# Chunk attention and a token-mixing MLP on one core: q and k loaded unit by unit with four rows in a partition, and one projection transposed in pairs of chunks

## The chip, the cores and the metric

The kernel runs on one core of one Trainium2 chip. The metric is the device time of one execution in microseconds (us). Before the change the median of three runs is 151.93 us (151.79 to 152.24). A further execution, the one whose profile is shown, took 152.53 us.

## What is computed

The inputs are q, k and v, each of 8 batches x 8 heads x 576 tokens x 64 columns in float32, and three weights: w_q and w_k (512 x 64) and w_out (512 x 512). The result is 8 x 576 x 512 in float32.

```python
# attention inside chunks of 64 tokens
scores = scale * np.matmul(q_c, k_c.transpose(0, 1, 2, 4, 3))
attn = softmax(scores)                 # with 1e-09 added to the sum
out = np.matmul(attn, v_c)
# then, with x = the heads side by side: batch x token x 512
wq, wk = x @ w_q, x @ w_k
W_tok = (1 / 8) * wq @ wk.T            # 576 x 576 per batch
result = np.maximum(W_tok @ x, 0.0) @ w_out
```

A head has nine chunks, a batch 72, and no chunk sees another. The MLP mixes all tokens of a batch; the kernel computes it as wq (wk^T x), so that the 576 x 576 matrix is never formed.

## The kernel before, in words

**Tiling.** The heads of a batch are split into two slabs of four heads. A slab fills 64 of the 128 partitions or 64 columns, so that two chunks, one of each slab, are worked on side by side. There are 36 such pairs of chunks in a batch (`NI`), and a *unit* is eight of them: 36 units (`NU`) in all, four and a half to a batch.

**Stages of a unit.** `stage_a1` transposes q and k on TensorE (PE) by 16 matmuls with an identity (line 375), so that the head's 64 columns come to lie on partitions; `stage_a2` copies the result from PSUM to SBUF on VectorE (DVE, line 385). `stage_b1` multiplies q by k (PE, line 400) and takes the maximum of each row (DVE, line 408); `stage_b2` subtracts it (DVE, line 414) and takes the exponential on ScalarE (ACT, line 422). `stage_c` transposes the result (PE, line 429; ACT copy, line 431). `stage_d1` multiplies by v, which has a column of ones for the sum (PE, line 445); `stage_d2` divides by the sum (DVE, lines 457, 459 and 460) and leaves a slice of x in SBUF.

**Rows in a partition.** q and k come with `R` = 2 neighbouring tokens in one partition (line 89): one contiguous piece of 128 float32 numbers in HBM becomes 128 float16 numbers in SBUF. The tokens of a chunk are thus held in the order (r g), r of 2 and g of 32, and not in their own order. That is undone for the keys where line 414 writes its result (`sh`, float32, as (g r)), and for the queries where the MLP's relu reads PSUM as (g r) (lines 267 and 287).

**Loads.** All loads are DMAs that GpSimd's queue (POOL) issues, because they cast from float32 to float16. `load_qk(b, part)` loads four or five of the nine half-units of a batch, with a DMA for each slab and each of q and k, so four DMAs. `load_v(b, part)` loads 8 or 10 of 18 chunk pairs with three DMAs (line 101) after a memset of the ones (line 98). Lines 119 to 125 issue two batches of q and k ahead of the first unit, with three parts of v among them. After that `reload` (line 506) issues the load of batch b + 2 when the same part of batch b has been used up; each part has two buffers. The weights come in behind the first reloads (`also`, line 501).

**Order.** The order on every engine is the order of the program. Lines 524 to 543 are the loop over units: in step kk, `stage_b1` of unit kk, `stage_d1` of unit kk - 2, `stage_a1` of unit kk + 2, `stage_c` of unit kk - 1, `stage_b2` of kk, `stage_d2` of kk - 2, `stage_a2` of kk + 2. The steps of a batch's MLP (`make_moe`) are put between them by a plan with places and costs (lines 472 to 498). One of them is `p_wkn` (line 204): it turns the projection wk, which lies as 64 rows x 576 tokens, by transposes of 64 x 64 (line 215), two for each of nine pairs of chunks, 18 in a batch. Slot n holds chunk 2n in partitions 0 to 63 and chunk 2n + 1, modulo nine, in partitions 64 to 127. After the last unit, lines 561 to 594 run what is left of batches 5, 6 and 7.

Of the kernel before, what the change touches and what calls it, by code (L numbers as in the profile page):

```python
# [9 lines left out]
F16 = mybir.dt.float16  # L10
# [7 lines left out]
def kernel(  # L18
# [12 lines left out]

    nc = tc.nc
    B, H, S, D = q.shape
    DM = moe_w_out.shape[0]
    DH = moe_w_q.shape[1]
    CH = 64
    P = 128
    HQ = H // 2  # L40
    NC_ = S // CH
    NI = HQ * NC_
    NT = NI // 4
    NS = NI // 2
    NU = B * NI // 8
    W0 = 5 * CH
    R, G = 2, 32
    scale_attn = 1.0 / math.sqrt(D)
    scale_moe = 1.0 / math.sqrt(DH)
    ds = bass.ds  # L50

    const = ctx.enter_context(tc.tile_pool(name="const", bufs=1))
    qn_pool = ctx.enter_context(tc.tile_pool(name="qn", bufs=2))
    v_pool = ctx.enter_context(tc.tile_pool(name="vpool", bufs=2))
    qkt_pool = ctx.enter_context(tc.tile_pool(name="qkt", bufs=3))
    sm_pool = ctx.enter_context(tc.tile_pool(name="smp", bufs=3))
# [14 lines left out]
    ident = const.tile([P, P], F16, name="ident")  # L71
# [5 lines left out]
    wqk16 = const.tile([P, HQ, 2 * DH], F16, name="wqk16")  # L77
    wout16 = const.tile([P, HQ, DM], F16, name="wout16")


    cuts = ((0, 4), (4, NT))
    v_cuts = ((0, 8), (8, NS))
    data = {}

    def load_qk(b, part):
        t0, t1 = cuts[part]
        for ti, x in enumerate((q, k)):
            tl = qn_pool.tile([P, 2, t1 - t0, R * D], F16, name=f"qn{ti}{part}", tag=f"qn{ti}{part}")
            of = x[b].rearrange("h s d -> (h s) d").rearrange("(l t p r) d -> l p t (r d)", l=2, p=P, r=R)
            for sl in range(2):  # L90
                nc.gpsimd.dma_start(tl[:, sl], of[sl, :, t0:t1, :])  # L91
            data[b, part, ti] = tl

    def load_v(b, part):
        n0, n1 = v_cuts[part]
        vt = v_pool.tile([P, 2, n1 - n0, D + 2], F16, name=f"vt{part}", tag=f"vt{part}")
        of = v[b].rearrange("h s d -> (h s) d").rearrange("(l n p) d -> l p n d", l=2, p=P)
        nc.gpsimd.memset(vt[:, :, :, D : D + 1], 1.0)

        for sl, to, at, rows in ((0, 0, 0, P), (1, 0, CH, CH), (1, CH, 0, CH)):  # L100
            nc.gpsimd.dma_start(vt[to : to + rows, sl, :, 0:D], of[sl, at : at + rows, n0:n1, :])  # L101
        data[b, part, 2] = vt
# [13 lines left out]

    load_qk(0, 0)
    load_qk(0, 1)  # L120
    load_v(0, 0)
    load_qk(1, 0)
    load_v(0, 1)
    load_qk(1, 1)
    load_v(1, 0)

    drain = [False]
    taken = [0]
# [1 line left out]
    def bank(shape, dtype, name):  # L130

        taken[0] += 1
        if drained() and taken[0] % 6 == 0:
            return s_psum.tile(shape, dtype, name=name, tag="sp")
        return m_psum.tile(shape, dtype, name=name, tag="m")

    def drained():
        return drain[0]

    def copy(on_vector, to, of):  # L140
        (nc.vector.tensor_copy if on_vector else nc.scalar.copy)(to, of)  # L141
# [9 lines left out]
    def make_moe(b):  # L151
# [52 lines left out]
        def p_wkn():  # L204


            wk = st["wqkT"][CH:P]
            wkn = moe_pool.tile([P, NC_, DH], F16, name="wkn", tag="wkn")

            cuts_ = (0, 5, NC_) if b == B - 1 else (0, NC_)  # L210
            for n0, n1 in zip(cuts_, cuts_[1:]):
                wp = bank([P, n1 - n0, DH], F16, name="wknp")
                for n in range(n0, n1):
                    for o in range(2):
                        nc.tensor.transpose(
                            wp[CH * o : CH * o + CH, n - n0, :],
                            wk[:, ds((2 * n + o) % NC_ * CH, CH)],
                            ident[CH:P, CH:P],
                        )
                copy(n0 > 0, wkn[:, n0:n1], wp[:])  # L220
            st["wkn"] = wkn
# [135 lines left out]
            outs.insert(0 if b == B - 1 else 4, (2, 0.9, p_out_tail))  # L357
        return xts[:2], chain, outs

    def batch_of(gj):  # L360
        return divmod(gj, NT)

    state = {}

    def stage_a1(u):

        tp = bank([P, 2, 2, 4, R, G], F16, name="tp")
        for j in range(2):
            b, t = batch_of(2 * u + j)
            for ti in range(2):  # L370
                part = t >= cuts[1][0]
                src = data[b, part, ti][:, :, t - cuts[part][0]]
                for r in range(R):
                    for sl in range(2):
                        nc.tensor.transpose(  # L375
                            tp[CH * sl : CH * sl + CH, j, ti, :, r, :],
                            src[:, sl, r * D : r * D + D],
                            ident[:],
                        )
        state[u] = {"tp": tp}  # L380

    def stage_a2(u):
        tp = state[u]["tp"]
        qkt = qkt_pool.tile([P, 2, 2, 4, R * G], F16, name="qkt", tag="qkt")
        nc.vector.tensor_copy(  # L385
            qkt[:].rearrange("p j t c k -> p (j t c k)"),
            tp[:].rearrange("p j t c r g -> p (j t c r g)"),
        )
        state[u]["qkt"] = qkt

    def stage_b1(u):


        qkt = state[u]["qkt"]
        sp = s_psum.tile([P, 8, CH], F32, name="sp", tag="sp")
        for i in range(8):
            j, c = divmod(i, 4)
            for sl in range(2):
                rows = slice(CH * sl, CH * sl + CH)
                nc.tensor.matmul(  # L400
                    sp[rows, i ^ sl, :],
                    lhsT=qkt[rows, j, 0, c, :],
                    rhs=qkt[rows, j, 1, c, :],
                    start=True,
                    stop=True,
                )
        mx = sm_pool.tile([P, 8], F32, name="mx", tag="mx")
        nc.vector.tensor_reduce(mx[:], sp[:], axis=AX.X, op=ALU.max)  # L408
        state[u]["sp"], state[u]["mx"] = sp, mx
# [24 lines left out]
    def stage_d1(u):  # L434
        et = state[u]["et"]
        xp = x_psum.tile([P, 2, 512], F32, name="xp", tag="xp")
        xv = xp[:, :, 0 : 4 * 65].rearrange("p l (m e) -> p l m e", e=65)
        for m in range(4):
            b, s = divmod(4 * u + m, NS)
            part = s >= v_cuts[1][0]  # L440
            vt = data[b, part, 2][:, :, s - v_cuts[part][0]]
            for sl in range(2):
                for par in range(2):
                    at = CH * (par ^ sl)
                    nc.tensor.matmul(  # L445
                        xv[CH * par : CH * par + CH, sl, m, :],
                        lhsT=et[at : at + CH, m, CH * sl : CH * sl + CH],
                        rhs=vt[at : at + CH, sl, 0 : D + 1],
                        start=True,
                        stop=True,  # L450
                    )
        state[u]["xv"] = xv
# [40 lines left out]
    def fill(kk, place, budget):  # L493
        spent = sum(run(x) for x in plan.pop((kk, place), []))
        while outs and outs[0][0] == place and spent + outs[0][1] <= budget:
            _, cost, step = outs.pop(0)
            step()
            spent += cost


    also = {
        (load_qk, 2, 0): [load_wqk, lambda: load_v(1, 1)],
        (load_qk, 2, 1): [load_wout],
    }

    def reload(load, unit, per_unit, per_batch, ends):

        for x in range(per_unit * unit + 1, per_unit * unit + per_unit + 1):
            b, end = divmod(x, per_batch)
            b, end = (b, end) if end else (b - 1, per_batch)  # L510
            for part in range(2):
                if end == ends[part][1] and b + 2 < B:
                    load(b + 2, part)
                    for more in also.pop((load, b + 2, part), ()):
                        more()

    def stage_a(u):
        stage_a1(u)
        reload(load_qk, u, 2, NT, cuts)
        stage_a2(u)  # L520

    stage_a(0)
    for kk in range(NU - 1):
        stage_b1(kk)
        if kk >= 2:
            stage_d1(kk - 2)
            reload(load_v, kk - 2, 4, NS, v_cuts)
        fill(kk, 0, 0.0)  # L530
        if 2 <= kk < NU - 2:
            stage_a1(kk + 2)
            reload(load_qk, kk + 2, 2, NT, cuts)
        if kk >= 1:
            stage_c(kk - 1)
        stage_b2(kk)
        if kk >= 2:
            stage_d2(kk - 2)
        if 2 <= kk < NU - 2:
            stage_a2(kk + 2)  # L540
        for u in ((1,), (2, 3))[kk] if kk < 2 else ():
            stage_a(u)
        fill(kk, 2, 1.4 if len(outs) < 4 else 1.9)
# [16 lines left out]

    u = NU - 1
    stage_b1(u)
    stage_d1(u - 2)
    stage_c(u - 1)
# [58 lines left out]
```

## Time and profile before

| what | value |
|---|---|
| the profiled execution | 152.53 us |
| its span, first to last instruction | 150.7 us, so 1.8 us lie around it |
| median of the three runs | 151.93 us, 0.60 us under the profiled one |
| mean granted clock of TensorE | 0.985 |
| DVE, `mx` of the first and the last unit (line 408) | 10.34 us and 122.10 us |
| POOL's last DMA issue begins | 103.4 us |
| packets of POOL's queue | 77152, 14.82 MB |

The engines are PE (matmul), PEld (weight load of PE), DVE, ACT, POOL and SP. POOL's busy time here is nearly all the making of DMAs; the transfers themselves run on 16 DMA engines. In a row of groups, the number after x is how often an instruction ran, then its busy time and its mean in ns, then how long the engine stood idle just before it and what ended that. In the timeline the first number is the start, the second the length, and brackets hold the idle time ahead of it. "Landing" is the time from the start of a DMA's issue to its last byte.

### The profile page before, as it was taken

Reading aid. Unit: us, or ns where it says so; the run is one execution under the profiler, and the core shown is the slowest. Engines: PE = TensorE matmul, PEld = TensorE weight load, DVE = VectorE, ACT = ScalarE, POOL = GpSimd, SP = SyncE. Lnnn points to the kernel's source line nnn. Section 1 sums busy time; section 2 is a strip of 40 time slices with the busy share of each in tenths; the row PEclk is TensorE's granted clock in tenths of the full one; section 3 lists DMA queues with packets and bytes.
Section 4 is the critical chain, followed back from the end, with each engine's and each line's share of the span. In section 5 each row is a group of like instructions: output and inputs, shape, how many; then the busy total and the mean of one; then the engine's idle time right before and its main releaser. Section 6 shows DMA issues by size and latency. Waiting matters only on the chain.

```text
span 150.7 us, 6041 instructions
## 1 busy us (share of the span) xinstructions
PE 122.2 (81%) x2580; PEld 83.0 (55%) x2580; DVE 113.9 (76%) x235; ACT 100.9 (67%) x199; POOL 94.3 (63%) x140
## 2 busy tenths in 40 slices
PE   0267767768686999998979999999879988999970
PEld 0156646556464775684747657766657655554430
DVE  0047997999989889998798899989968897454530
ACT  3004334556658979996888899979986996777130
POOL 8999999999789999968878996986000000000000
PEclk9999995999999999999999999999999999999998
DMA  1999999999999999999999999999922344334484
GB/s 17 147 156 163 163 162 165 113 145 145 168 181 166 167 172 192 199 211 212 255 203 217 173 205 220 229 189 244 214 54 74 73 154 157 112 139 106 177 255 165
DMA packets 83050, 25.08 MB, mean 166 GB/s; under 512 B 77392, under 2 KB 78544, under 8 KB 83024
## 3 DMA queue, kind: packets, MB, share of 16 engines
q0 software_dynamic: 77152, 14.82, 118.1%
q1 hardware_dynamic: 5728, 9.75, 19.1%
q8 instruction: 20, 0.33, 0.9%
q10 hardware_dynamic: 144, 0.13, 0.3%
q14 instruction: 6, 0.05, 0.1%
HBM read 29.62 MB, written 9.44 MB: 259 GB/s over the span
## 4 chain that ended last, share of the span: by engine, by line
PE 40%; DVE 16%; ACT 13%; POOL 12%; DMA 11%; issue 5%; DVEq 0%; ACTq 0%; POOLq 0%
PE op L313 11%; POOL qn L91 8%; DMA qn<-in_k_dram 8%; PE tp L375 5%; DVE x_nat L460 4%; DVE sh L414 4%; PE ep L429 4%; DMA out_dram<-osb 3%; ACT es L422 3%; DVE mx L408 3%; POOL vt L101 3%; ACT osb L141 3%; PE tx L165 3%; DVE qkt L385 3%; PE sp L400 3%
## 5 line engine op out<-in xcount | busy, mean ns | idle before, releaser
L101 POOL DMA_DIRECT2D vt<-in_v_dram x48 | 37.9, 824 | 5.6 <-DMA vt<-in_v_dram 3.1
L431 ACT COPY et<-ep 128x512 f16<-128x512 f16 x36 | 21.4, 595 | 18.5 <-PE ep L429 17.2
L375 PE MATMUL tp<-ident,qn 128*64 128x128 f16 x576 | 26.8, 235 | 8.5 <-DMA qn<-in_q_dram 6.1
L385 DVE COPY qkt<-tp 128x1024 f16<-128x1024 f16 x36 | 24.5, 682 | 9.2 <-PE tp L375 9.1
L313 PE MATMUL op<-wout,rmx 128*128 128x512 f16 x124 | 30.5, 379 | 0.2 <-ACT rmx L147 0.2
L422 ACT ACTIVATE es<-sh 128x512 f16<-128x512 f32 x36 | 23.3, 646 | 10.1 <-DVE sh L414 10.1
L408 DVE TENSOR_REDUCE mx<-sp 128x8 f32<-128x512 f32 x36 | 24.7, 686 | 6.8 <-PE sp L400 6.7
L91 POOL DMA_DIRECT2D qn<-in_k_dram x32 | 26.5, 862 | 3.0 <-PE ep L429 1.1
L375 PEld LDWEIGHTS <-qn 128*64 128x64 f16 x576 | 20.4, 118 | 13.1 <-DMA qn<-in_q_dram 6.5
L414 DVE TENSOR_TENSOR sh<-sp,mx 128x512 f32<-128x512 f32 x36 | 24.9, 692 | 3.5
L91 POOL DMA_DIRECT2D qn<-in_q_dram x32 | 27.1, 881 | 0.5 <-issue 0.4
L460 DVE TENSOR_TENSOR x_nat<-xp,rec 128x512 f16<-128x512 f32 x36 | 24.9, 692 | 1.2
L141 ACT COPY osb<-op 128x512 f32<-128x512 f32 (+1 forms) x29 | 17.1, 598 | 7.1 <-PE op L313 5.6
L400 PEld LDWEIGHTS <-qkt 64*64 64x64 f16 x576 | 12.6, 113 | 15.8 <-issue 5.3
L400 PE MATMUL sp<-qkt 64*64 64x64 f16 x576 | 16.8, 200 | 5.0 <-DVE sh L414 2.1
L445 PE MATMUL xp<-vt,et 64*64 64x65 f16 x576 | 13.2, 198 | 7.3 <-DVE x_nat L460 3.6
L141 ACT COPY xt<-tx 128x768 f16<-128x768 f16 (+1 forms) x23 | 18.2, 792 | 0.9 <-PE tx L165 0.9
L313 PEld LDWEIGHTS <-rmx 128*128 128x128 f16 x124 | 11.2, 98 | 10.2 <-issue 0.6
L147 ACT ACTIVATE rmx<-ma 128x512 f16<-128x512 f32 x28 | 15.4, 610 | 1.1 <-PE ma L251 1.0
L429 PE MATMUL ep<-ident,es 128*128 128x128 f16 x144 | 14.7, 226 | 0.0
L445 PEld LDWEIGHTS <-et 64*64 64x64 f16 x576 | 9.4, 108 | 9.2 <-ACT es L422 5.1
L165 PE MATMUL tx<-ident,x_nat 128*128 128x128 f16 x144 | 12.3, 223 | 0.0
(47 smaller groups left out, 139.9 us busy)
## 6 DMA issues: line engine op xcount, KB each, us to landing
out_dram<-osb SPq DMA_DIRECT2D x31, 256.0 KB, 4.1
qn<-in_q_dram POOLq DMA_DIRECT2D x16, 160.0 KB, 5.5
qn<-in_k_dram POOLq DMA_DIRECT2D x16, 160.0 KB, 5.9
qn<-in_q_dram POOLq DMA_DIRECT2D x16, 128.0 KB, 6.2
qn<-in_k_dram POOLq DMA_DIRECT2D x16, 128.0 KB, 5.9
vt<-in_v_dram POOLq DMA_DIRECT2D x8, 160.0 KB, 6.9
vt<-in_v_dram POOLq DMA_DIRECT2D x16, 80.0 KB, 5.9
out_dram<-osb SPq DMA_DIRECT2D x9, 128.0 KB, 3.0
```

The source lines that it names most:

```text
L91: nc.gpsimd.dma_start(tl[:, sl], of[sl, :, t0:t1, :])
L101: nc.gpsimd.dma_start(vt[to : to + rows, sl, :, 0:D], of[sl, at : at + rows, n0:n1, :])
L141: (nc.vector.tensor_copy if on_vector else nc.scalar.copy)(to, of)
L313: nc.tensor.matmul(op[:], lhsT=rmx[:, i, ds(t * P, P)], rhs=wout16[:, i, :], start=(i == 0), stop=(i == HQ - 1),)
L375: nc.tensor.transpose(tp[CH * sl : CH * sl + CH, j, ti, :, r, :], src[:, sl, r * D : r * D + D], ident[:],)
L385: nc.vector.tensor_copy(qkt[:].rearrange("p j t c k -> p (j t c k)"), tp[:].rearrange("p j t c r g -> p (j t c r g)"),)
L400: nc.tensor.matmul(sp[rows, i ^ sl, :], lhsT=qkt[rows, j, 0, c, :], rhs=qkt[rows, j, 1, c, :], start=True, stop=True,)
L408: nc.vector.tensor_reduce(mx[:], sp[:], axis=AX.X, op=ALU.max)
L414: nc.vector.tensor_tensor(out=sh[:].rearrange("p i (g r) -> p i r g", g=G, r=R), in0=sp[:].rearrange("p i (r g) -> p i r g", g=G, r=R), in ...
L422: nc.scalar.activation(es[:], sh[:], AF.Exp, scale=scale_attn)
L445: nc.tensor.matmul(xv[CH * par : CH * par + CH, sl, m, :], lhsT=et[at : at + CH, m, CH * sl : CH * sl + CH], rhs=vt[at : at + CH, sl, 0 : ...
L460: nc.vector.tensor_tensor(out=x_nat[:, 4 * u : 4 * u + 4, :, :].rearrange("p m l d -> p l m d"), in0=xv[:, :, :, 0:D], in1=rec[:, :, :, No ...
```

## The change

q and k now have `R` = 4 tokens in a partition and `G` = 16, so one contiguous piece is 256 float32 numbers. `load_qk(u)` loads one unit: one DMA of 128 partitions for q and one for k, each with both slabs. Nine units make two batches; the fifth of the nine (w = 4) straddles both and takes two DMAs of 64 partitions for each of q and k. There are ten buffers: ten units are issued ahead of the first, with the three parts of v behind units 3, 6 and 8, and then unit u + 10 when `stage_a1` of unit u has been issued. The weights and the fourth part of v follow units 11 and 13. The order of v's reloads stays.

`stage_a1` makes the same 16 transposes, by q and k, r and slab. `stage_a2`, `stage_b1`, lines 414, 267 and 287 keep their shapes but for the indices: the inner dimensions are 4 x 16 in place of 2 x 32. In `p_wkn` both chunks of a pair are transposed at once, 64 x 128, but for slot 4 (chunks 8 and 0); that makes 10 transposes in place of 18.

```diff
-    R, G = 2, 32
+    R, G = 4, 16
-    qn_pool = ctx.enter_context(tc.tile_pool(name="qn", bufs=2))
+    qn_pool = ctx.enter_context(tc.tile_pool(name="qn", bufs=10))
...
-    cuts = ((0, 4), (4, NT))
+    AHEAD = 10
-    def load_qk(b, part):
-        t0, t1 = cuts[part]
+    def load_qk(u):
+        pair, w = divmod(u, 9)
+        if w == 4:
+            pieces = ((2 * pair, 32, 0, CH), (2 * pair + 1, 0, CH, CH))
+        else:
+            odd = int(w > 4)
+            pieces = ((2 * pair + odd, 8 * w - NI * odd, 0, P),)
         for ti, x in enumerate((q, k)):
-            tl = qn_pool.tile([P, 2, t1 - t0, R * D], F16, name=f"qn{ti}{part}", tag=f"qn{ti}{part}")
-            of = x[b].rearrange("h s d -> (h s) d").rearrange("(l t p r) d -> l p t (r d)", l=2, p=P, r=R)
-            for sl in range(2):
-                nc.gpsimd.dma_start(tl[:, sl], of[sl, :, t0:t1, :])
-            data[b, part, ti] = tl
+            tl = qn_pool.tile([P, 2, R * D], F16, name=f"qn{ti}", tag=f"qn{ti}")
+            for b, i0, p0, pn in pieces:
+                of = x[b].rearrange("h s d -> (h s) d").rearrange("(l p r) d -> p l (r d)", l=2, r=R)
+                at = i0 * G
+                nc.gpsimd.dma_start(tl[p0 : p0 + pn], of[at : at + pn])
+            data[u, ti] = tl
...
-    load_qk(0, 0)
-    load_qk(0, 1)
-    load_v(0, 0)
-    load_qk(1, 0)
-    load_v(0, 1)
-    load_qk(1, 1)
-    load_v(1, 0)
+    for u in range(AHEAD):
+        load_qk(u)
+        if u in (3, 6, 8):
+            load_v(*{3: (0, 0), 6: (0, 1), 8: (1, 0)}[u])
...
-                    for o in range(2):
+                    halves = ((0, CH), (CH, P)) if n == NC_ // 2 else ((0, P),)
+                    for lo, hi in halves:
+                        at = (2 * n * CH + lo) % S
                         nc.tensor.transpose(
-                            wp[CH * o : CH * o + CH, n - n0, :],
-                            wk[:, ds((2 * n + o) % NC_ * CH, CH)],
-                            ident[CH:P, CH:P],
+                            wp[lo:hi, n - n0, :], wk[:, at : at + hi - lo], ident[CH:P, CH:P]
                         )
...
-    also = {
-        (load_qk, 2, 0): [load_wqk, lambda: load_v(1, 1)],
-        (load_qk, 2, 1): [load_wout],
-    }
+    also = {11: [load_wqk, lambda: load_v(1, 1)], 13: [load_wout]}
+    def reload_qk(u):
+        if u + AHEAD < NU:
+            load_qk(u + AHEAD)
+            for more in also.get(u + AHEAD, ()):
+                more()
```

## The prediction, made before the changed kernel was run

> **What bounds the kernel now.** I read the page's busy times and slices first, then the timeline from the start, the waits, the groups with shapes kept apart, and the chain. From the page:
>
> ```profile
> PE 122.2 (81%) x2580; PEld 83.0 (55%) x2580; DVE 113.9 (76%) x235; ACT 100.9 (67%) x199; POOL 94.3 (63%) x140
> DVE  0047997999989889998798899989968897454530
> POOL 8999999999789999968878996986000000000000
> ```
>
> DVE fills nine tenths of most slices from the fourth to the thirty-second; POOL, which issues the loads, fills its own from the first. Three stretches have three limits. *The start*, to `mx` of unit 0 at 10.34 us, waits for loads:
>
> ```profile
> 4.72 0.31 PE L375 MATMUL tp<-ident,qn 128*64 128x128 f16 x1 [4.72 <-DMA qn<-in_q_dram]
> ...
> 8.03 0.85 PE L375 MATMUL tp<-ident,qn 128*64 128x128 f16 x11 [0.62 <-DMA qn<-in_k_dram]
> 8.91 0.69 DVE L385 COPY qkt<-tp 128x1024 f16<-128x1024 f16 x1 [8.91 <-PE tp L375]
> ...
> 10.34 0.69 DVE L408 TENSOR_REDUCE mx<-sp 128x8 f32<-128x512 f32 x1 [0.73 <-PE sp L400]
> ```
>
> Unit 0 uses two of the four pieces of a 512-token load, yet waits for all four DMAs of q and k: their landings end waits at 4.72, 6.37, 7.09 and 8.03. *The loop*, to 122.10, has DVE's step as its floor: the group rows give 682 (line 385), 686 (408), 692 (414), 692 (460), 203 and 157 ns, 3.11 us in sum, and `mx` follows `mx` by 3.03 us in 15 of the 35 steps, since neighbours overlap a little. 35 such steps are 106.1 us; the loop took 111.8. *The end*, 28 us, is the MLP of the last batches, where POOL issues nothing. Of the loop's loss one step is a load's, between `mx` at 22.07 and 25.79, 3.72 us:
>
> ```profile
> 23.57 0.42 PE L375 MATMUL tp<-ident,qn 128*64 128x128 f16 x3 [0.81 <-DMA qn<-in_k_dram]
> ```
>
> The others come after ACT's and PE's MLP steps and after six gaps of 0.4 to 1.0 us on PE marked "issue", at 42.13, 48.27, 71.21, 77.75, 105.97 and 112.73.
>
> **The start.** Unit 0 now needs two DMAs, each of the same 128 KB as one of the four before (half as many pieces of twice the size). Their landing took 3.2 and 4.0 us from issue in the before, the second's at 6.33. The second now starts no later than 2.33 and lands by 6.3: the gain on the fourth (7.98) is 1.7, and 0.1 more if the first issue is shorter (0.65 for 0.88, below): **-1.8 us**. Bounds: -1.2 (larger pieces land a half microsecond later) and -2.6 (both land like the first, 3.2 after issue). What follows is in time by the same counting: unit 1's pair lands near 7.7, before its turn; the first part of v is issued by 8.2 and lands, 4.3 later, at 12.5, wanted at 15.7 - 1.8 = 13.9.
>
> **The stall at unit 5** (-0.7, from 3.72 - 3.03). Before, batch 1's second part must land whole, at 23.5. Counting DMAs in POOL's new order, unit 6's k is the 16th of q and k, with three of v before it, and is issued by about 14 us; with the 5.4 us that v and k take there it lands near 19, and PE wants it at 22.07 - 1.8 = 20.3. The stall goes; bounds -0.7 and 0.
>
> **What POOL pays.** q and k have 64 DMAs now and 80 after (32 units x 2 + 4 x 4). Start to start, POOL needs 0.74 us for 128 partitions of four pieces (line 91), 0.85 for five, 0.88 and 0.94 for eight and ten of v, and for 64 partitions 0.68 and 0.71 (eight and ten) and 0.60 (four, `wqk`):
>
> ```profile
> 25.07 0.62 POOL L111 DMA_DIRECT2D wqk<-in_moe_w_k_dram  x1
> 25.67 0.63 POOL L110 DMA_DIRECT2D wqk<-in_moe_w_q_dram  x1
> ```
>
> So it is mostly a price per DMA. For 128 partitions of two pieces the step from eight to four leads to 0.67, that from five to four to 0.52; I take 0.65, nearest to `wqk` with as many pieces, and 0.56 for 64 partitions (0.50 to 0.60). A unit costs 1.30, nine units 8 x 1.30 + 4 x 0.56 = 12.6, against 8 x 0.74 + 8 x 0.85 = 12.7 for two batches before. **POOL saves nothing.** Q and k also run ten units ahead in place of nine, so what stands behind them is later. The fourth part of v comes behind units 0 to 11: 22 x 0.65 + 4 x 0.56 = 16.5 us of q and k, where before 20 DMAs took 15.9 (6.5 + 3.0 + 3.4 + 3.0). Its last DMA begins at 29.2 instead of 28.6 and lands, with the 4.5 us of before, at 33.7. Line 445 of unit 6 wants it at 34.5 - 2.5 = 32.0; DVE reads the result 1.4 us after PE could start (den at 36.27, PE at 34.51 for 0.32), so 0.3 is left. The same sum for the second v part of batch 2, the tightest later one: last issue 43.5, landing 5.6 later at 49.1, wanted at 50.7 - 2.5 + 1.4 = 49.6: nothing. I take **+0.4** for v; bounds 0 (steps of 0.52) and 4.0 (0.74 and landings of 7 us; rival 2).
>
> A second limit of POOL shows in its waits:
>
> ```profile
> POOL vt L101 <- DMA vt<-in_v_dram: 3.1, 5, 0.7
> POOL vt L101 <- DMA qn<-in_k_dram: 1.4, 1, 1.4
> ```
>
> Each of these ends when the eighth DMA before it has landed (40.60 waits for line 115's at 33.30). With eight under way, 0.65 holds while a landing takes under 5.2 us.
>
> **The DMA engines.** q and k are 36864 pieces now and 18432 after. For equal bytes, 128 KB in pieces of 256 B follow each other by 0.75 us in landing, 256 KB of v in 128 B by 1.83, 256 KB of `wout` in 1 KB by 1.36. Between the first and the last, 128 KB in 512 B take 0.68 to 0.71. That is 36 x 2 x 0.05 = 3.6 us of transfer, beside work nearly everywhere; it keeps landings from growing, and I count 0 for it (bounds 0 and -1).
>
> The Trainium skill, "DMA: Bandwidth & Descriptors", Rules for kernel authors, speaks against the split fifth unit: two transfers to disjoint partition halves serialize, use one of 128 partitions. By rows, the four such units cost POOL 4 x (4 x 0.56 - 2 x 0.65) = 3.8 us; that is already in the sum.
>
> **Transposes of wk.** 18 become 10 in each of eight batches. Before, 18 last 0.44 us where PE's queue is full and 0.68 where ACT released them, as here on the chain:
>
> ```profile
> 80.69 0.68 PE wknp L215 x18
> ```
>
> The last matmul takes 0.19, so each of the others sets the pace at (0.68 - 0.19)/17 = 29 ns there, and at (0.44 - 0.19)/17 = 15 ns where the queue is full. Eight fewer at 29 ns save 0.23 at each of the three places of 0.68 on the chain, -0.7. But 128 columns of weights, not 64, may load longer: line 429's four loads of 128 columns take 0.23 in all and 0.10 for one, 43 ns apart. Ten at 43 are 0.43, against 18 x 29 = 0.52 and 18 x 15 = 0.27: -0.09 three times and +0.16 five times, +0.5. I take **-0.3**, nearer to the first, as the weights here have 64 rows and their matmuls 64 columns; bounds -0.7 and +0.5.
>
> **Edits with a price of nothing.** The 16 transposes of a unit write 32 B runs to PSUM instead of 64 B; line 375's median of 219 ns at 64 B stands beside line 429's mean of 226 with 256 B: 0, and at most another 20 ns on each of 16, 36 x 0.3 beside DVE's floor. The relus read PSUM with a step of 64 B instead of 128 B; 610 ns against 606 for the contiguous copy of the same size: 0. `sh` is written with a step of 16 B instead of 8 B. Line 414 costs what line 460 costs, which writes contiguous runs:
>
> ```profile
> L414 DVE TENSOR_TENSOR sh<-sp,mx 128x512 f32<-128x512 f32 x36 | 24.9, 692 | 3.5
> L460 DVE TENSOR_TENSOR x_nat<-xp,rec 128x512 f16<-128x512 f32 x36 | 24.9, 692 | 1.2
> ```
>
> The nearest row is line 414 itself, so 0 (no gain either: line 460's contiguous write is no faster). The upper bound is the row twice, 36 x 0.69 = 25 us, paid in full, as DVE is the floor.
>
> On this the Trainium skill, "Advanced Engine Details and Errata", Memory Cachelines, has a rule against the change: SBUF lines are 16 B and two hits on a line are needed to avoid a penalty. At 8 B there are two hits, at 16 B one. No row here writes with that step; by the rule line 414 would be longer by an amount that the page does not give.
>
> **The sum.** -1.8 - 0.7 + 0.4 - 0.3 = **-2.4 us**, on the profiled execution 152.53 to 150.1. The median is 0.60 under that execution: 151.93 - 2.4 = **149.5 us**. The loop's floor and the end stay.
>
> **Rivals.** 1. *More is gained* (0.11): 147.0 to 148.4. The gaps marked "issue" on PE made five units late by 0.1 to 1.4 us; if they come from full DMA engines, fewer pieces shorten them by 1 to 2.5 us. For: five of the six lie where loads run. Against: the loads go on at the same bytes.
> 2. *The wait moves to v* (0.11): slower. POOL's step stays 0.74 although the pieces halve, and landings take 7 us as at 35 us in the before. Then 32 x 0.74 + 8 x 0.60 = 28.5 in place of 25.3 puts that v part of batch 2 at 43.5 + 3.2 + 7.0 = 53.7 against 50.7 + 1.4: 1.6 later than before, less 0.3 for wk, 153.2. It decides from a step of about 0.72 on with landings above 6 us. Against: 0.60 for `wqk`.
> 3. *The start's gain is given back, without loss* (0.12): the same with landings of 5.6; the loop is held at v's old times, 151.0 to 152.3.
> 4. *`sh` gets slower* (0.09): each 67 ns on line 414 costs 2.4 us and takes the gain; from there it decides, up to 151.9 - 2.4 + 25 = 174. Against: the equal rows.
>
> **Chances.** Forecast (148.4 to 150.9) 0.57, rivals as given. What a measurement can tell is about 0.3%, 151.5 to 152.4. Faster: 0.57 + 0.11 + 0.05 of rival 3 = 0.73; same 0.07 of rival 3 and 0.01 of rival 2 = 0.08; slower 0.10 + 0.09 = 0.19. The range goes from inside rival 1 to the end of rival 2, 147.2 to 153.2, and leaves out rival 4.
>
> **What the profile would show.** Right: first `mx` near 8.5; no gap at unit 5; 3.03 between `mx` and 692 on line 414; 80 issues of q and k some 0.65 apart; 58976 packets on POOL's queue (55296 + 1536 of the weights + 16 for each of 134 DMAs); line 215 at 10 per batch; PE with 64 matmuls fewer; last `mx` near 119.7. Wrong: PE waiting at line 445 for `vt` at units 6 to 13; line 414 above 700; line 375 above 240.

## The result and the profile after

The changed kernel takes 158.69 us (median of four, 158.34 to 159.83) against 152.09 (151.79 to 153.18) of the kernel before: ratio 1.043, 95% interval 1.036 to 1.051. A forecast of 2.4 us less met 6.6 us more. Medians here are of all executions; a ratio leaves out those that were disturbed, so it can differ a little from that of two medians. The profiled execution took 158.75 us with a span of 157.0; line numbers move by a few (414 is now 411, 445 is 442, 91 is 97, 101 is 107, 215 is 221).

From the page of the changed kernel, the busy times, POOL's queue, the chain's shares by engine, and the group that the prediction priced at nothing:

```profile
PE 128.9 (82%) x2516; PEld 88.5 (56%) x2516; DVE 124.2 (79%) x235; ACT 102.4 (65%) x199; POOL 97.9 (62%) x156
...
q0 software_dynamic: 58976, 14.82, 100.2%
...
DVE 43%; PE 20%; POOL 20%; DMA 6%; issue 4%; ACT 3%; DVEq 0%; ACTq 0%; POOLq 0%
...
L411 DVE TENSOR_TENSOR sh<-sp,mx 128x512 f32<-128x512 f32 x36 | 38.8, 1078 | 3.6
```

The packets are 58976, as counted. But the subtraction that writes `sh` takes 1078 ns in place of 692, DVE is 10.3 us busier although it does the same 235 instructions, and the chain, which was PE's for 40%, is DVE's for 43%.

The start, from DVE's timeline of the changed kernel:

```profile
7.38 0.69 DVE L383 COPY qkt<-tp 128x1024 f16<-128x1024 f16 x1 [7.38 <-PE tp L373]
8.80 0.69 DVE L405 TENSOR_REDUCE mx<-sp 128x8 f32<-128x512 f32 x1 [0.73 <-PE sp L397]
9.53 1.05 DVE L411 TENSOR_TENSOR sh<-sp,mx 128x512 f32<-128x512 f32 x1
```

The first `mx` comes at 8.80 instead of 10.34. In the middle, the chain's list shows DVE alone, one instruction behind the other:

```profile
61.07 0.61 DVE mx L405
...
61.77 1.09 DVE sh L411
...
63.15 0.69 DVE x_nat L457
63.84 0.60 DVE qkt L383
64.44 0.61 DVE mx L405
```

From `mx` to `mx` it is 3.37 us, where it was 3.03. So the three stretches are: the start 1.54 us shorter (8.80 for 10.34); the loop, from the first to the last `mx`, 119.24 for 111.76, 7.48 longer; the end 28.94 for 28.55, 0.39 longer. That is 6.33, which is the difference of the two spans. Thirty-five steps that are 0.34 longer make 11.9 us; the loop lost less because its stalls, mostly the MLP's and 5.7 us over the floor before, are now mostly hidden behind the slower DVE: 1.3 over the new floor.

### The profile page after: what moved, and what is told of

It is laid out like the page before. It is cut to its first block, busy times and chain, and to the rows that moved or that the text cites. A ratio compares the mean times of both kernels' runs of the same rounds, so it can differ in the third digit from the quotient of the medians.

```text
span 157.0 us, 5961 instructions
## 1 busy us (share of the span) xinstructions
PE 128.9 (82%) x2516; PEld 88.5 (56%) x2516; DVE 124.2 (79%) x235; ACT 102.4 (65%) x199; POOL 97.9 (62%) x156
## 3 DMA queue, kind: packets, MB, share of 16 engines
q0 software_dynamic: 58976, 14.82, 100.2%
## 4 chain that ended last, share of the span: by engine, by line
DVE 43%; PE 20%; POOL 20%; DMA 6%; issue 4%; ACT 3%; DVEq 0%; ACTq 0%; POOLq 0%
DVE sh L411 15%; POOL qn L97 12%; DVE x_nat L457 9%; DVE mx L405 8%; PE op L317 8%; DVE qkt L383 6%; DMA vt<-in_v_dram 6%; POOL vt L107 5%; DVE rec L456 3%; PE wknp L221 2%; PE tp L373 2%; ACT osb L144 1%; PE tx L168 1%; PE opt L334 1%; PE xp L442 1%
## 5 line engine op out<-in xcount | busy, mean ns | idle before, releaser
L411 DVE TENSOR_TENSOR sh<-sp,mx 128x512 f32<-128x512 f32 x36 | 38.8, 1078 | 3.6
L107 POOL DMA_DIRECT2D vt<-in_v_dram x48 | 38.5, 865 | 2.6 <-issue 2.1
L97 POOL DMA_DIRECT2D qn<-in_k_dram x40 | 30.6, 779 | 4.2 <-PE ep L426 1.9
L97 POOL DMA_DIRECT2D qn<-in_q_dram x40 | 31.3, 795 | 2.3 <-PE xp L442 1.2
L373 PEld LDWEIGHTS <-qn 128*64 128x64 f16 x576 | 21.3, 124 | 10.3 <-DMA qn<-in_q_dram 4.8
L397 PEld LDWEIGHTS <-qkt 64*64 64x64 f16 x576 | 13.2, 117 | 16.2 <-issue 5.6
L397 PE MATMUL sp<-qkt 64*64 64x64 f16 x576 | 17.4, 205 | 5.0 <-DVE den L454 2.7
L442 PEld LDWEIGHTS <-et 64*64 64x64 f16 x576 | 10.2, 112 | 14.1 <-ACT es L419 6.7
L426 PE MATMUL ep<-ident,es 128*128 128x128 f16 x144 | 15.5, 236 | 0.0
L168 PE MATMUL tx<-ident,x_nat 128*128 128x128 f16 x144 | 13.3, 234 | 0.0
```

What stands on the lines that cost most here:

```text
L97: nc.gpsimd.dma_start(tl[p0 : p0 + pn], of[at : at + pn])
L373: nc.tensor.transpose(tp[CH * sl : CH * sl + CH, ti, :, r, :], src[:, sl, r * D : r * D + D], ident[:],)
L397: nc.tensor.matmul(sp[rows, i ^ sl, :], lhsT=qkt[rows, 0, i, :], rhs=qkt[rows, 1, i, :], start=True, stop=True,)
L411: nc.vector.tensor_tensor(out=sh[:].rearrange("p i (g r) -> p i r g", g=G, r=R), in0=sp[:].rearrange("p i (r g) -> p i r g", g=G, r=R), in ...
L442: nc.tensor.matmul(xv[CH * par : CH * par + CH, sl, m, :], lhsT=et[at : at + CH, m, CH * sl : CH * sl + CH], rhs=vt[at : at + CH, sl, 0 : ...
```

## The experiments

Theory A: DVE's float32 write with a step of 16 B is slow, and sets the loop's pace. Theory B: the inner run of 16 elements, in place of 32, is what costs. Theory C: the loads are the cause. To which comes, once A's part is taken away, the question why the start's gain does not show. "Before" is the kernel before on the same chip.

**1. The exponential puts the keys in order.**

```diff
-            out=sh[:].rearrange("p i (g r) -> p i r g", g=G, r=R),
+            out=sh[:].rearrange("p i (r g) -> p i r g", g=G, r=R),
...
-        nc.scalar.activation(es[:], sh[:], AF.Exp, scale=scale_attn)
+        nc.scalar.activation(
+            es[:].rearrange("p i (g r) -> p i r g", g=G, r=R),
+            sh[:].rearrange("p i (r g) -> p i r g", g=G, r=R),
+            AF.Exp,
...
```

> The changed kernel, but the subtraction writes sh contiguously in the order (r g), and the exponential on ACT puts the keys back in order by writing es (float16) with a step of 8 B. Theory A (the 16 B step of DVE's float32 write is what costs): line 411 falls from 1078 to about 692 ns, DVE's step from 3.37 to 3.03 us, and the time to 149.5 to 151.5 us, the prediction's sum with v's wait a little larger. Theory B (the short inner run of 16 elements costs, whichever engine walks it): line 411 is fast, but the exponential grows from 633 ns by a like 0.3 us; ACT has room, so the time is near 151 as well. Theory C (the loads are the cause and sh only fills the wait): the time stays at 157 to 159.

165.69 us, ratio 1.087 (1.077 to 1.096): none of the theories had that. In its groups, by line:

```profile
L419 ACT ACTIVATE es<-sh 128x512 f16<-128x512 f32 x36 | 49.3, 1369 | 7.2 <-DVE sh L411 7.0
...
L411 DVE TENSOR_TENSOR sh<-sp,mx 128x512 f32<-128x512 f32 x36 | 24.9, 692 | 3.5
```

DVE's line is back at 692, so C is out as the cause of its length; but ACT's write of float16 with a step of 8 B costs 1369 ns for 633. The cost went with the strided write to the other engine, and there the step of 8 B, harmless on DVE in float32, is dear on ACT in float16 (experiment 4 parts engine and type). A and B both still stand.

**2. The subtraction reads PSUM with the step and writes contiguously.**

```diff
-            out=sh[:].rearrange("p i (g r) -> p i r g", g=G, r=R),
-            in0=sp[:].rearrange("p i (r g) -> p i r g", g=G, r=R),
+            out=sh[:].rearrange("p i (g r) -> p i g r", g=G, r=R),
+            in0=sp[:].rearrange("p i (r g) -> p i g r", g=G, r=R),
```

> The changed kernel, but the subtraction walks in the order (g r): it reads PSUM with a step of 64 B in runs of 4 and writes sh contiguously. Theory A: 692 ns at line 411, and the time of the kernel in which the exponential reorders, within 0.7 us. Theory B (short runs): runs of 4 are worse than runs of 16, line 411 at 1078 ns or above, and the time above 158. Theory C: 157 to 159 whatever line 411 takes.

```profile
L411 DVE TENSOR_TENSOR sh<-sp,mx 128x512 f32<-128x512 f32 x36 | 24.9, 692 | 3.5
```

Line 411 takes 692 ns with runs of 4 elements that lie 64 B apart in PSUM. B is out: shorter runs, no cost. The time is 155.97 us, ratio 1.014 (0.999 to 1.028); on another chip, beside experiment 9, 156.30 and 1.019 (1.012 to 1.026).

> The changed kernel with line 411 writing contiguously alone, beside the one with v earlier on the same chip. What is between them is v's place (about 3 us by the runs so far) and the transposes (about 1.2 us): 3 to 5 us, and 1 to 2% over the kernel before.

So A holds for 2.4 to 3.0 points of the 4.3 (about 4 us), and the rest of the change is not the gain that was forecast but a loss of some 2 to 3 us (the first interval alone would still allow none).

**3. The kernel before, with a step of 16 B.** `sh` gets a gap after each element; R stays 2.

```diff
-        sh = sm_pool.tile([P, 8, CH], F32, name="sh", tag="sh")
+        sh = sm_pool.tile([P, 8, CH, 2], F32, name="sh", tag="sh")
...
-            out=sh[:].rearrange("p i (g r) -> p i r g", g=G, r=R),
+            out=sh[:, :, :, 0].rearrange("p i (g r) -> p i r g", g=G, r=R),
```

> The kernel before, with R = 2 and its runs of 32, but sh has a gap after each element, so that the subtraction writes with a step of 16 B (and the exponential reads with a step of 8 B). Theory A: line 414 at about 1078 ns, and 6 to 9 us more than before, 158 to 161. Theory B (run length): 692 ns and 152. Theory C: 152.

157.64 us, ratio 1.034 (1.026 to 1.042), and in its groups:

```profile
L414 DVE TENSOR_TENSOR sh<-sp,mx 128x512 f32<-128x512 f32 x36 | 38.7, 1076 | 3.6
```

The write step, in the old kernel with its old loads and runs of 32, brings the same 1.08 us and most of the loss. The exponential now reads with a step of 8 B, but that is not what costs: it takes 664 ns for 646, and `mx` follows `mx` by 3.36 us as in the changed kernel. The expected 6 to 9 us were 5.1: the loop takes 116.98 us and 35 steps of 3.36 are 117.6, so the MLP's stalls are hidden here too.

**4. The step by itself.** Behind the stores of the kernel before stand three each of subtractions and exponentials of 128 x 512 with all steps; its time has no meaning.

```diff
+    for _ in range(3):
+        nc.vector.tensor_tensor(out=big[:].rearrange("p a b -> p (a b)")[:, 0 : 2048 : 4], in0=pt[:], in1=st32[:], op=ALU.subtract)
```

> The kernel before with 3 subtractions each added after its stores, 128 x 512 from PSUM, whose writes step 4, 8, 12, 16, 32 and 64 B (float32) and 2, 4, 8, 16 and 32 B (float16), then reads of SBUF at 8, 16 and 64 B, and the same on ACT. Its time has no meaning. Theory A (one element per 16 B line is slow for a write): DVE float32 at 692 ns to 8 B, near 1080 from 16 B on; float16 the same by bytes, near 692 at 8 B. The exponential that wrote float16 at 8 B took 1369 ns, so for ACT the step from which it is slow must be 8 B or less. If the number of runs mattered and not the step, all of these, one run each, stay at 692.

From its groups, shapes apart. `big` is float32, `bigh` float16; lines 609, 611, 613 and 615 write with steps of 8, 12, 16 and 32 B, lines 621, 623 and 625 with 4, 8 and 16 B; line 639 is ACT at 16 B, line 631 a DVE read of SBUF at 16 B:

```profile
L625 DVE TENSOR_TENSOR bigh<-ptile,st 128x512 f16<-128x512 f32 x3 | 7.3, 2422 | 0.1
...
L623 DVE TENSOR_TENSOR bigh<-ptile,st 128x512 f16<-128x512 f32 x3 | 3.9, 1293 | 0.1
...
L615 DVE TENSOR_TENSOR big<-ptile,st 128x512 f32<-128x512 f32 x3 | 3.2, 1074 | 0.1
L639 ACT ACTIVATE big<-ptile 128x512 f32<-128x512 f32 x3 | 3.2, 1066 | 0.1
...
L631 DVE TENSOR_TENSOR st32b<-big,st 128x512 f32<-128x512 f32 x3 | 3.2, 1060 | 0.1
L613 DVE TENSOR_TENSOR big<-ptile,st 128x512 f32<-128x512 f32 x3 | 3.2, 1057 | 0.1
...
L611 DVE TENSOR_TENSOR big<-ptile,st 128x512 f32<-128x512 f32 x3 | 2.5, 832 | 0.1
...
L621 DVE TENSOR_TENSOR bigh<-ptile,st 128x512 f16<-128x512 f32 x3 | 2.2, 726 | 0.1
L609 DVE TENSOR_TENSOR big<-ptile,st 128x512 f32<-128x512 f32 x3 | 2.1, 691 | 0.1
```

A float32 write costs 670 ns without a step, 691 at 8 B, 832 at 12 B and 1057 at 16 B, and no more beyond (1074 at 32 B, 1015 at 64 B). Two float32 elements in 16 B are nearly free, one is not: theory A in its own numbers. The expectation for float16 was wrong: 726 at 4 B, but 1293 already at 8 B, with two elements in 16 B, and 2422 at 16 B. ACT does the same: 619 in float32 at 8 B, 1302 in float16.

**5. The transposes of wk alone, in the kernel before.** The edit is the change's own, lines 213 to 219 of the kernel before.

> The kernel before with the transposes of wk by pairs alone, 10 in place of 18 in a batch. The prediction's step: -0.3 us, bounds -0.7 and +0.5. If the wider weight load decides, the chain's pieces of 0.68 us stay and those of 0.44 grow by 0.16: +0.5.

154.79 us against 153.11, ratio 1.010 (0.997 to 1.023): by time it tells nothing. Experiment 8 asks again.

**6. What is left of the change: the loads and R = 4.** Experiment 2 with the 18 transposes of before:

```diff
-                            wp[lo:hi, n - n0, :], wk[:, at : at + hi - lo], ident[CH:P, CH:P]
+                            wp[CH * o : CH * o + CH, n - n0, :],
+                            wk[:, ds((2 * n + o) % NC_ * CH, CH)],
+                            ident[CH:P, CH:P],
```

> The kernel in which line 411 reads PSUM with the step and writes contiguously, with the transposes of wk as before the change (18). What is left of the change is the loads and R = 4. If v behind ten units of q and k gives the start back: first mx near 7.6, waits of PE on vt at units 5, 9 and 12, last mx within 1.5 us of 122.1, and a time within 1.5 us of the kernel before. If v's place costs nothing: 2.5 us faster than before. Against the same with 10 transposes: 0.2 us less per batch, about 1.2 us less in all.

154.02 us, ratio 1.011 (1.006 to 1.016). The first `mx` comes at 7.41, 2.9 us earlier than before, and the last at 122.84, 0.7 later. Its waits (us in all, how many, the longest) say where the gained 3.7 us went, and its chain (start and length in us) names one place:

```profile
PE tp L373 <- DMA qn<-in_q_dram: 6.8, 2, 4.7
...
PE xp L442 <- DMA vt<-in_v_dram: 5.9, 6, 1.8
```

```profile
31.09 4.33 DMA vt<-in_v_dram
35.42 0.04 issue
35.47 0.32 PE xp L442 x6
```

PE waits 5.9 us for v in all, in a line that never waited for v before. The fourth part of v, the one that the prediction put at 33.7, is issued at 31.09 and lands at 35.4, and the step between `mx` there is 8.01 us long, 5.0 over the floor. PE's two waits for v in it are 1.21 and 1.82 us. The rest is PE's own pace: from 35 to 40 us its granted clock is 0.52, and what follows, up to the next scores, takes 4.09 us where the same work takes 2.21 in experiment 7 at a clock of 1.00. The first 16 transposes of it, here and there:

```profile
35.72 1.07 PE L373 MATMUL tp<-ident,qn 128*64 128x128 f16 x16
```

```profile
32.37 0.64 PE L373 MATMUL tp<-ident,qn 128*64 128x128 f16 x16
```

Why the clock fell there is not shown.

**7. v earlier.** The same, with q and k seven units ahead and v and the weights moved up:

```diff
-    AHEAD = 10
+    AHEAD = 7
-        if u in (3, 6, 8):
-            load_v(*{3: (0, 0), 6: (0, 1), 8: (1, 0)}[u])
+        if u in (3, 5):
+            load_v(*{3: (0, 0), 5: (0, 1)}[u])
-    also = {11: [load_wqk, lambda: load_v(1, 1)], 13: [load_wout]}
+    also = {7: [lambda: load_v(1, 0)], 9: [lambda: load_v(1, 1)], 10: [load_wqk], 12: [load_wout]}
```

> The same, but q and k run seven units ahead, and v's parts and the weights are issued that much earlier (v's first behind unit 3, its second behind unit 5, its third behind unit 7, its fourth behind unit 9, w_q and w_k behind unit 10, w_out behind unit 12). If v's place in POOL's queue is what gives the start back, the waits on vt at units 9 and 12 go and most of the one at unit 5, and the time is 2 to 3 us under the kernel before: 149 to 150.5. If the DMA engines' pace is what holds v, it lands no earlier and the time is that of the kernel with ten ahead.

151.04 us, ratio 0.989 (0.983 to 0.995), beside the kernel of experiment 6 on the same chip: 2.2 points, 3.3 us, for the places of the same loads in the queue. Under the kernel before it is 1.7 us, where 2 to 3 were expected. A part of the 3.3 can be the clock's, but not all: executions of experiment 6 at mean clocks of 0.976 and 0.989 took 152.92 and 152.79 us, those of this kernel at 0.977 and 0.985 took 150.85 and 150.40, 2.1 to 2.4 less. Its waits:

```profile
PE tp L373 <- DMA qn<-in_q_dram: 7.2, 5, 4.6
...
PE tp L373 <- DMA qn<-in_k_dram: 1.5, 3, 0.7
...
PE xp L442 <- DMA vt<-in_v_dram: 0.2, 1, 0.2
```

The waits of PE for v are down from 5.9 us to 0.2. Its waits for q and k are 8.7 us in all, 4.6 of them the first load; the longest of the rest is 1.3 us, up to 44.3, behind w_out, which has landed at 43.2.

**8. The same with 10 transposes of wk.**

> The kernel with v earlier, with the 10 transposes of wk by pairs as in the change. If the wider weight load sets their pace (0.65 us for 10 against 0.45 for 18 in the traces so far), it is 1.0 to 1.6 us slower than the one with 18. The prediction's step (-0.3) wants it 0.3 faster.

152.15 us, ratio 1.000 (0.997 to 1.004), where 18 transposes gave 0.989: the pairs cost 1.1 points, about 1.7 us. The traces of before and after, PE's timeline at the seventh batch, show a part of why:

```profile
127.69 0.47 PE L215 MATMUL wknp<-ident,wqkT 64*64 64x64 f16 x18
```

```profile
133.71 0.65 PE L221 MATMUL wknp<-ident,wqkT 64*128 64x64 f16 x10
```

Ten take 0.64 to 0.66 us in seven of the eight batches of the changed kernel, 0.76 in the other; 18 took 0.45 to 0.68. Over the eight batches that is 5.3 us of PE for 4.7. Where the rest of the 1.7 us comes from is not shown.

**9. The faster kernel again.**

> The kernel with v earlier (seven units ahead, w_out behind unit 12, 18 transposes, line 411 writing contiguously) once more, on whatever chip comes: 1.1% under the kernel before the first time (0.983 to 0.995). If that gain holds across chips, 0.98 to 1.00 again; if w_q and w_k landing late as in the kernel with w_out later (2.3 us of wait) is a matter of the chip, PE waits for them here too and the gain is gone.

151.83 us against 152.72, ratio 0.985 (0.978 to 0.993), on another chip; the medians alone give 0.994, since the ratio takes three of this kernel's six executions. The gain has the same sign both times, its size is not sure. Experiment 2's kernel on that chip is at 1.019. Between the ratios lie 3.4 points, v's place and the transposes together.

**10. w_out behind unit 16, and nine units ahead.** Two variants of experiment 7: `12: [load_wout]` becomes `16: [load_wout]`, and, with that, `AHEAD = 9` with v in the same places among the first units.

> The kernel with v earlier (seven units ahead), with w_out (512 KB) behind unit 16 in place of unit 12. In that kernel's profile PE waits for q at 44.3 and k at 51.3, 1.8 us together, behind w_out's transfer. If w_out is what made them late, these waits go and the time falls by about 1 us, to 150; if it is the pace of POOL and the DMA engines in general, they stay.

154.53 us, ratio 1.007 (1.001 to 1.013). The waits at 44 and 51 went, but this profile has others:

```profile
PE wpa L186 <- DMA wqk<-in_moe_w_k_dram: 2.3, 1, 2.3
...
PE op L317 <- DMA wout<-in_moe_w_out_dram: 1.4, 1, 1.4
```

w_out now comes late for its own use, by 1.4 us. That w_q and w_k came 2.3 us late in the same place of the queue as in experiment 7, where nothing waited for them, was not foreseen. The profile of experiment 9, with experiment 7's order on a third chip, has no such wait either; why it came here the runs do not settle.

> Nine units ahead again, but v's parts in the same places among the units as in the kernel with v earlier, and w_out behind unit 16. The order among the first units is the same; later parts of v (batch 2 on) stand behind two units more. If only the order of the first 12 units matters, it is as fast as with seven ahead; if each unit more ahead of v's reloads costs POOL's 1.4 us, PE waits for vt near 45 and 52 and it is 1 to 2 us slower.

156.02 us, ratio 1.018 (1.005 to 1.031):

```profile
PE tp L373 <- DMA qn<-in_q_dram: 6.3, 3, 4.7
...
PE xp L442 <- DMA vt<-in_v_dram: 5.1, 3, 3.2
```

Two units more ahead of v's reloads bring the waits for v back, at 42.5 and 51.9, as the second expectation said, and for more than it said.

## Why the prediction was wrong, step by step

- **`sh` at no price: the step that failed.** The row at 8 B was taken as the nearest for 16 B, and the term put at 0. The price is 386 ns, 36 times, 13.9 us of DVE; 5.1 us of time alone (experiment 3), about 4 us in the change (1.043 against 1.014 and 1.019). The upper bound of 25 us held it, the chance of 0.09 did not weigh it. The two equal rows, line 460's contiguous float16 and line 414's float32 at 8 B, say nothing of float32 at 16 B, since the cost sets in between: 691 at 8 B, 832 at 12, 1057 at 16. Rival 4's mechanism was right and its price was not: by its 2.4 us for each 67 ns, "paid in full", 386 ns would be 13.8 us, and the runs show 4 to 5, since the slower DVE hides stalls that it waited for before.
- **The page's rule.** The Trainium skill, "Advanced Engine Details and Errata", Memory Cachelines, asks for two hits on a line of 16 B. For float32 the runs agree: 691 ns at 8 B, 1057 from 16 B on, and 832 at 12 B in between. For float16 they differ: two hits at 8 B cost 1293 ns on DVE and 1302 on ACT, so there the measurement decides, and only 4 B was nearly free.
- **The start, -1.8:** -1.5 in the changed kernel's profile, within the bounds; -2.5 to -2.9 in the nine profiles of experiments 1, 2 and 6 to 10, whose first loads are the same, mostly past the bound of -2.6. Mechanism right; the size goes with the landing of the second DMA, 4.4 us in the changed kernel's profile and 3.0 to 3.4 in the eight others that recorded it. The subtraction comes after the first `mx` and has no part in it.
- **The stall at unit 5, -0.7:** right for that step in the changed kernel, where it is 3.35, the new floor; it is 3.03 in experiments 6 and 9, and 4.16 in experiment 7, where PE waits 0.8 us for q and its clock is 0.50 from 20 to 25 us. But with the first units earlier PE waits for q at another place, 2.1 us up to 15.2 in experiment 6 and 1.3 up to 14.7 in experiment 9, which the sum did not have.
- **v behind ten units, +0.4:** mechanism right, size wrong. POOL's step is 0.71 and 0.59 (start to start) in place of 0.65 and 0.56: 22 x 0.71 + 4 x 0.59 = 18.0, not 16.5, and the last DMA of v's fourth part begins at 30.8, not 29.2. Its landing at 35.0 was put at 33.7. The order costs up to 3.3 us (experiment 6 against 7, the clock's part included), within the bound of 4.0. What rival 3 described, the start's gain given back, is there in experiment 6, which ends its loop 0.7 us later than before; it came together with rival 4, and the prediction had priced each by itself alone.
- **The transposes, -0.3:** wrong in sign, +1.7. The concern that wider ones follow each other more slowly was right, and 43 ns was too little: (0.65 - 0.19)/9 is 51 ns from one to the next, against 15 to 29 for the 64 x 64 ones. What sets this pace is not shown: one weight load of 64 x 128 takes 96 ns, one of 64 x 64 takes 108. The prediction read 0.44 us for 18 at the five other places; the timeline has 0.45 to 0.63 there. Nor were these places quite without effect: the end of the kernel, where two of them lie, takes 28.94 us with ten and 28.78 in experiment 6 with 18.
- **Priced at nothing and rightly so:** the relus (610 before and after), the transposes to PSUM in 32 B runs (the median is 219 ns before and after; the mean is 244 against 235, with the clock lower in stretches). Landings of q and k fell from a median of 5.5 to 6.2 to one of 4.7 us with fewer pieces; no time could be seen from it.

## What to carry to other kernels

A strided write from DVE or ACT is priced by its own step and type, not by the nearest row with another step: float32 was slow from 12 B on, float16 already at 8 B. Measure the step itself before giving a permutation to an engine that sets the pace, and let the strided side be the read from PSUM, which cost nothing here. A load that is made smaller and issued further ahead shifts everything behind it in the same queue; list what is due when, count the queue's price per DMA, and issue in the order of need. Fewer and larger matmuls are no gain in themselves: ten transposes of 64 x 128 took longer here than 18 of 64 x 64.

## What the runs showed of the hardware that was not expected

- The granted clock of TensorE fell to a half in stretches of the start. From the table of stretches of the changed kernel (start:end, length, then busy time and count of PE, PEld, DVE, ACT and POOL, then the clock):

```profile
20.00:25.00 5.00, 4.28 (x92) 3.57 (x94) 4.72 (x12) 2.27 (x4) 5.00 (x9) 0.50 1.69 165
...
35.00:40.00 5.00, 4.99 (x72) 3.85 (x71) 3.20 (x7) 2.45 (x6) 5.00 (x9) 0.50 1.11 144
```

  In the second, 72 matmuls fill PE, and the step between `mx` there is 5.08 us; the work that takes 4.09 us in experiment 6 at such a clock, and 2.21 in experiment 7, takes 4.09 here too. PE had stood idle for no longer than 1.5 us at a time since its first load. The kernel before had 0.83 from 20 to 30 us and 1.00 in all other stretches up to 120. It does not carry the verdict: the four executions of the changed kernel had mean clocks of 0.933 to 0.985, and the one at 0.985 took 158.62 us. What makes it fall, and what it adds to the time of each kernel, was not tried alone.
- POOL has no more than eight DMAs under way: before and after, an issue that waits for a DMA ends its wait when the eighth before it has landed. Whether the chip or the program's own semaphores set that is not shown.
